# Reading the moving columns of TensorE's matmuls in pairs from both halves, in a float32 attention and feed-forward kernel

## The chip, the cores and the metric

The kernel runs on one core of a Trainium2 chip. The metric is the device time of one execution in microseconds (us). A core has TensorE (PE in the profile; its weight loads stand apart as PEld), VectorE (DVE), ScalarE (ACT), GpSimd (POOL, almost unused here) and SyncE (SP), whose queue issues nearly all DMAs.

## What is computed

```
# q, k, v: (8, 12, 448, 64) float32
scores = q @ k^T / sqrt(64) - log(448)
attn   = 1 / (1 + exp(-scores))                    # sigmoid, no normalisation over keys
x      = (attn @ v), heads side by side            # (3584 tokens, 768)
h      = x @ w_in                                  # 768 -> 2048
g      = s * max(h, 0)**2 + b
out    = g @ w_out                                 # 2048 -> 768
```

All of it is float32. w_in and w_out reach the kernel as 64-bit words, which it converts itself.

## The kernel before

**Precision.** A product of two float32 operands is made from two rounded parts of each, a high and a low part of type float32r, by three matmuls (`PARTS`: high by high, high by low, low by high). A float32r matmul is one record in the trace. Where plain float32 tiles go into a matmul (attention times v, the last 64 keys' scores, the first scores of all), one matmul is two records.

**Attention** runs over 24 steps of `quads`, each with four heads of one batch. `scores` (L420, L426) makes six tiles of 128 keys: the keys are the stationary operand and the 448 queries the moving one, two heads side by side on the two halves of the array's rows. `scores_last` (L441) does the remaining 64 keys for the next step. ACT takes each tile through the sigmoid into an SBUF tile `a`. `attn_v` (L454) and `attn_v_last` (L463) multiply by v, with v stationary and `a` moving, into the PSUM tile `pav`. `store_x` (L470) copies `pav` with DVE, and SP stores it to DRAM as x. `pav` has one buffer, which it shares with the score tile (0, 2) of the next step, the fourth tile in the order in which a step makes them. Beside this, DVE and ACT convert weights, split q and k into parts, and prepare sums of weight blocks, by a plan of numbered steps.

**The first block of 512 tokens** goes through the feed-forward part directly: `ffn1` (L563) and `ffn2` (L765), 18 matmuls each, 16 times in turn, with `activate` on ACT between them. Six PSUM tiles `pos` gather the output and ACT copies them out.

**The other six blocks** are taken three at a time (`threes`), by a scheme of 15 products in place of 18 for a 3 x 2 by 3 x 3 product of blocks. For each of the two groups, a first list of 60 units (L1095: 12 matmuls of 512 columns each) makes sums of h; after each unit `results_1` adds or copies a PSUM tile into the tiles `G`, which are squared and scaled; a second list of 60 units (L1225, again 12 matmuls each) multiplies sums of `G` by sums of w_out; `results_2` (L1138 on) takes each of the 15 finished PSUM tiles into the output tiles `C`, from which SP stores the output. A unit's weights `wu` are fetched from DRAM six units ahead. The last unit is split in three (`LAST`): 512 tokens of one tile, then twice 256 tokens of the other, each with its own subtraction and store.

The order on each engine is written out by hand (the program text is the order); tiles and their releases add the waits. PSUM has four tiles of two banks in the last part, in turn.

**Columns.** In all of these matmuls the moving operand is a row of consecutive 4-byte columns in each partition: `x[r, i, 0, :]`, `two[xi][r, i, :S]`, `x0[h][xi][:, cc, :]`, `g[:, gi, :]`, `opd[i][xi][:, c, :]` and `g[gi][:, f, tk]`. PSUM gets the result's columns in the same order, and so does every tile behind it.

Of the kernel before, what the change touches and what calls it, by code (L numbers as in the profile page):

```python
# [36 lines left out]
TB = 512  # L37
# [57 lines left out]
def sigmoid_attention_relu2_ffn(  # L95
# [10 lines left out]
    nc = tc.nc  # L106
# [66 lines left out]

    def f32(ap):
        return ap.bitcast(F32)

    def add(o, x, y):
        nc.vector.tensor_tensor(o, x, y, op=ALU.add)  # L178

    def sub(o, x, y):  # L180
        nc.vector.tensor_tensor(o, x, y, op=ALU.subtract)  # L181
# [221 lines left out]
    def scores(b, t, ld_):  # L403
        x = ld_[0]
        two = ld_.pop() if len(ld_) > 2 else None
        whole = two is None or (b, t) == quads[0]
        a = {}
        psc = {}
        order = [(i, c) for i in range(2) for c in range(3)]
        if not whole:  # L410
            order[2:4] = order[3], order[2]
        for i, c in order:

            pl, tag = (ps_av, "pav") if (i, c) == (0, 2) else (ps_qk, "psc")
            o = psc[i, c] = pl.tile([P, 2, 512], F32, tag=tag, name=f"psc_{b}_{t}_{i}_{c}")
            if two and (i or not whole):
                cols = slice(S + c * P, S + (c + 1) * P)
                for m, (wi, xi) in enumerate(PARTS):
                    for j, r in enumerate(half):
                        nc.tensor.matmul(  # L420
                            o[:, j, :S], two[wi][r, i, cols], two[xi][r, i, :S],
                            start=m == 0, stop=m == 2,
                        )
            else:
                for j, r in enumerate(half):
                    nc.tensor.matmul(  # L426
                        o[:, j, :S], x[r, i, 1, c * P : (c + 1) * P], x[r, i, 0, :],
                        start=True, stop=True,
                    )
            if not whole and (i, c) == (1, 0):  # L430
                continue
            for k in [(i, c)] + [(1, 0)] * (not whole and (i, c) == (0, 2)):
                a[k] = sigmoid(psc[k], f"{b}_{t}_{k[0]}_{k[1]}")
        return a

    def scores_last(b, t, ld_):
        x = ld_[0]
        psc = ps_qk.tile([P, 2, 512], F32, tag="psc", name=f"psc_{b}_{t}_l")
        for j, r in enumerate(half):
            for i in range(2):  # L440
                nc.tensor.matmul(  # L441
                    psc[half[i], j, :S], x[r, i, 1, 3 * P :], x[r, i, 0, :],
                    start=True, stop=True,
                )
        return sigmoid(psc, f"{b}_{t}_l")
# [21 lines left out]

    def store_x(b, t, pav):
        o = xo.tile([P, 2, S], F32, tag="xo", name=f"xo_{b}_{t}")
        nc.vector.tensor_copy(o, pav[:, :, :S])  # L470
        nc.sync.dma_start(x_dram[b][:, 2 * t : 2 * t + 2], o)

    loaded = {0: load(*quads[0], first=True)}
# [82 lines left out]
    def ffn1(f, w):  # L556
        ph = ps_h.tile([P, TB], F32, tag="ph", name=f"ph_{f}")
        m = 0
        for c in range(NCC):
            h, cc = divmod(c, HC)  # L560
            k, kc = divmod(c, KC)
            for wi, xi in PARTS:
                nc.tensor.matmul(  # L563
                    ph, w[:, k, wi, kc * P : (kc + 1) * P], x0[h][xi][:, cc, :],
                    start=m == 0, stop=m == 3 * NCC - 1,
                )
                m += 1
        cx.free(w)
        return ph
# [191 lines left out]
    def ffn2(w, g, first, last):  # L761
        for e in range(NCC) if not last else evict:
            k, kc = divmod(e, KC)
            for i, (wi, gi) in enumerate(PARTS):
                nc.tensor.matmul(  # L765
                    pos[e], w[:, k, wi, kc * P : (kc + 1) * P], g[:, gi, :],
                    start=first and i == 0, stop=last and i == 2,
                )

# [73 lines left out]
    outs = []  # L843
    for e in evict[::2]:
        outs.append(slot(f"o_{e}"))
        nc.scalar.copy(outs[-1][:, 0], pos[e])
        nc.scalar.copy(outs[-1][:, 1], pos[e + 1])
    todo[10].pop(0)()
    blk_ps.close()
    ps = pool(ctx, "ps", 4, space=PSUM)  # L850
# [100 lines left out]
    for n, blocks in enumerate(threes):  # L951
# [128 lines left out]
        for u, (i, p) in enumerate(L1):  # L1080
            wt = weights()
            if n == 0 and u < 4:
                load_raw(0, *start[5 + u])
            if outs and u > 4:
                out_store(outs[0], evict[6 - 2 * len(outs)], 0, 2)
                heap.free(outs.pop(0))
            ch = next(c for c in CHAINS_1 if i in c)
            if i == ch[0]:
                banks[p] = ps.tile([P, 2, TB], F32, tag="b", name=f"h_{n}_{i}_{p}")
            bk = banks[p]  # L1090
            for j in range(2):
                m = 0
                for c in range(KC):
                    for wi, xi in PARTS:
                        nc.tensor.matmul(  # L1095
                            bk[:, j], wt[:, j, wi, c * P : (c + 1) * P], opd[i][xi][:, c, :],
                            start=i == ch[0] and m == 0,
                            stop=m == 3 * KC - 1,
                            skip_group_check=True,
                        )  # L1100
                        m += 1
            if p == NPP - 1:
                for t in opd.pop(i):
                    heap.free(t)
                for key in {3: ("3",), 13: ("13",), 2: ("2",), 9: ("9",), 5: ("10",), 0: ((0, 2),),
                            12: ((1, 1),), 11: ((1, 2),), 14: ((2, 0),)}.get(i, ()):
                    A.pop(key)
            here = places.get(u, ())
            casts = []
            for q_ in (10,) * (n == 0 and u < 2) + here:  # L1110
                fn = todo[q_].pop(0)
                if u < 4 and fn.__name__ == "hi":
                    casts.append(fn)
                else:
                    fn()
            if u >= len(L1) - LEAD:
                prep(u - len(L1) + LEAD)
            ready, scales = scales, []
            for _ in range(2 - len(here)):
                if later:  # L1120
                    later.popleft()()
            results_1(i, p, bk)
            for fn in casts + ready:
                fn()
            for f, units in LATER_SUMS.items() if n == 0 else ():
                for _ in range(units.count(u)):
                    next(later_sums_[f], None)
# [8 lines left out]
        later = collections.deque()  # L1136

        def results_2(i, bk):  # L1138
            def copy(c):
                C[c] = slot(f"C_{n}_{c}")  # L1140
                nc.scalar.copy(C[c], bk)

            def put(c, keep=False):
                m, k = divmod(c, 3)
# [8 lines left out]
            elif i == 6:  # L1153
                copy(5)
            elif i == 10:
                sub(C[5], C[5], bk)
                put(5)
            elif i == 7:
                C[2] = slot(f"C_{n}_2")
                sub(C[2], C["u"], bk)  # L1160
                copy(0)
                put(2)
            elif i == 1:
                sub(C[0], bk, C[0])
                put(0)
            elif i == 2:
                copy(7)
            elif i == 5:
                copy(8)
            elif i == 4:  # L1170
                sub(C[8], bk, C[8])
            elif i == 3:
                sub(C[7], C[7], bk)
                put(7, True)
            elif i == 12:
                C[1] = C.pop("u")
                sub(C[1], bk, C[1])
                put(1)
            elif i == 11:
                C[3] = slot(f"C_{n}_3")  # L1180
                sub(C[3], C["t"], bk)
                put(3)
            elif i == 14:
                copy("v")
            elif i == 0:
                sub(C["v"], C["v"], bk)

                def eight():
                    add(C[8], C[8], C["v"])
# [9 lines left out]
            elif n + 1 < len(threes):  # L1199
                C[4] = C.pop("t")  # L1200
                for e in range(KC):
                    sub(C[4][:, e], C[4][:, e], bk[:, e])
                    m, k = divmod(4, 3)
                    out_store(C[4][:, e : e + 1], KC * k + e, blocks[m], 1)
                heap.free(C.pop(4))
# [4 lines left out]
        for j, (i, p) in enumerate(L2):  # L1210
# [8 lines left out]
            for e, tk in LAST if end else [(e, slice(TB)) for e in range(KC)]:  # L1219
# [3 lines left out]
                for f in range(2):  # L1223
                    for m, (wi, gi) in enumerate(PARTS):
                        nc.tensor.matmul(  # L1225
                            o, wt[:, f, wi, e * P : (e + 1) * P], g[gi][:, f, tk],
                            start=(end or i == ch[0] and p == 0) and f == 0 and m == 0,
                            stop=p == NPP - 1 and f == 1 and m == 2,
                            skip_group_check=True,
                        )  # L1230
                if end:
                    x = C["t"][:, e, tk]
                    sub(x, x, o)
                    t0 = blocks[1] * TB
                    nc.sync.dma_start(
                        out[(KC + e) * P : (KC + e + 1) * P, t0 + tk.start : t0 + tk.stop], x
                    )
            if n + 1 == len(threes) and j + 2 == len(L2):
                sub(C["t"], C["t"], bk)
            for t in g:  # L1240
                heap.free(t)
            if j in loads:
# [47 lines left out]
```

## Time and profile before

| what | value |
|---|---|
| median of 3 runs | 1039.26 us (1038.59 to 1039.77) |
| span of the profiled execution, first to last instruction | 1037.5 us |
| what lies between that span and the median | 1.8 us |
| ACT busy | 617.2 us (59%) |
| DMA | 287.16 MB, mean 277 GB/s |
| granted TensorE clock, mean | 1.000 |

The profiled execution's time is given by its span alone. "Busy" is time in which an engine had an instruction in it; a matmul's record is longer than the distance to the next, because matmuls are pipelined, so for TensorE the distance between starts counts. A row of a timeline gives the start, the length of the whole group, the engine, the line, what is written and read, the partitions and columns, and how many instructions it merges.

### The profile page before, as it was taken

The numbers are of one execution on the slowest core, as the hardware profiler recorded it, in microseconds if no ns is written. First come the engines' busy times: TensorE is split into PE (matmuls) and PEld (weight loads), VectorE is DVE, ScalarE is ACT, GpSimd is POOL, SyncE is SP. The second block draws the span as 40 slices with busy tenths as digits, with TensorE's granted clock in tenths as the row PEclk, the third lists the DMA queues.
The fourth block names the chain that finished last, engine by engine and source line by source line (L and its number), as shares of the span: only waits on it lengthen the run. The fifth ranks groups of instructions, "written<-read, shape, count | busy, mean of one in ns | idle before, by whom it ended". The sixth has DMA issues, their size and how long they took to land.

```text
span 1037.5 us, 13898 instructions
## 1 busy us (share of the span) xinstructions
PE 1033.7 (100%) x5288; PEld 780.3 (75%) x5288; DVE 836.1 (81%) x906; ACT 617.2 (59%) x666; POOL 0.2 (0%) x4
## 2 busy tenths in 40 slices
PE   9999999999999999999999999999999999999998
PEld 4545555555888888888888888888888888888887
DVE  5999999995988965898898897796455789888777
ACT  7999999988776755564445344344445335552432
POOL 0000000000000000000000000000000000000000
PEclk9999999999999999999999999999999999999999
DMA  9788989995999999999686676897666666676773
GB/s 327 269 331 342 360 317 393 346 396 194 332 366 367 358 408 410 341 341 322 201 269 189 218 229 220 291 317 249 197 190 195 194 193 197 190 236 207 222 228 118
DMA packets 101568, 287.16 MB, mean 277 GB/s; under 512 B 10240, under 2 KB 20352, under 8 KB 101504
## 3 DMA queue, kind: packets, MB, share of 16 engines
q1 hardware_dynamic: 101216, 285.84, 79.6%
q8 instruction: 42, 0.69, 0.3%
q10 hardware_dynamic: 288, 0.46, 0.1%
q14 instruction: 22, 0.18, 0.0%
HBM read 198.18 MB, written 88.08 MB: 276 GB/s over the span
## 4 chain that ended last, share of the span: by engine, by line
PE 100%; DVE 0%; issue 0%
PE o L1225 31%; PE h L1095 31%; PE pav L454 11%; PE psc L420 9%; PE ph L563 6%; PE po L765 6%; PE psc_l L441 2%; PE pav L463 2%; PE psc L426 0%; PE idle L482 0%; DVE C_t L181 0%
## 5 line engine op out<-in xcount | busy, mean ns | idle before, releaser
L1095 PE MATMUL h<-s_1h,wu 128*128 128x512 f32 x480 | 148.0, 389 | 0.0
L1095 PE MATMUL h<-s_0h,wu 128*128 128x512 f32 x480 | 147.8, 389 | 0.0
L400 ACT ACTIVATE a<-psc,nls 128x896 f32<-128x896 f32 x144 | 132.7, 1008 | 12.9 <-PE psc L420 10.1
L454 PE MATMUL pav<-a,v 128*64 128x448 f32 x576 | 113.8, 543 | 0.0
L1095 PEld LDWEIGHTS h<-s_1h,wu 128*128 128x128 f32 x480 | 90.1, 188 | 18.8
L1095 PEld LDWEIGHTS h<-s_0h,wu 128*128 128x128 f32 x480 | 90.1, 188 | 18.6
L968 ACT COPY G<-h 128x1024 f32<-128x1024 f32 x48 | 48.8, 1017 | 85.5 <-PE h L1095 57.8
L860 ACT ACTIVATE G<-G,b_sb,s_sb 128x1024 f32<-128x1024 f32 x48 | 59.8, 1246 | 61.4 <-DVE G L857 60.7
L1095 PE MATMUL h<-s_0l,wu 128*128 128x512 f32 x240 | 93.4, 389 | 0.0
L1095 PE MATMUL h<-s_1l,wu 128*128 128x512 f32 x240 | 93.4, 389 | 0.0
L454 PEld LDWEIGHTS pav<-a,v 128*64 128x64 f32 x576 | 39.1, 137 | 63.8 <-issue 45.4
L178 DVE TENSOR_TENSOR G<-G,h 128x1024 f32<-128x1024 f32 x40 | 48.8, 1219 | 39.4 <-PE h L1095 39.3
L1225 PE MATMUL o<-g_3h,wu 128*128 128x512 f32 (+1 forms) x244 | 79.0, 385 | 0.0
L1225 PE MATMUL o<-g_0h,wu 128*128 128x512 f32 x240 | 78.8, 389 | 0.0
L1225 PE MATMUL o<-g_1h,wu 128*128 128x512 f32 x240 | 78.8, 389 | 0.0
L1225 PE MATMUL o<-g_2h,wu 128*128 128x512 f32 x240 | 78.8, 389 | 0.0
L765 PE MATMUL po<-g,w 128*128 128x512 f32 x288 | 67.7, 389 | 0.0
L765 PEld LDWEIGHTS po<-g,w 128*128 128x128 f32 x288 | 54.1, 188 | 11.2
L563 PE MATMUL ph<-x0h,w 128*128 128x512 f32 x192 | 61.7, 390 | 0.0
L420 PE MATMUL psc<-qkh 64*128 64x448 f32 x282 | 54.1, 380 | 0.0
L1225 PEld LDWEIGHTS o<-g_3h,wu 128*128 128x128 f32 x244 | 45.6, 188 | 9.2
L1095 PEld LDWEIGHTS h<-s_0l,wu 128*128 128x128 f32 x240 | 45.0, 188 | 9.4
(152 smaller groups left out, 2028.0 us busy)
## 6 DMA issues: line engine op xcount, KB each, us to landing
wu<-wd SPq DMA_DIRECT2D x240, 512.0 KB, 3.6
wd<-t SPq DMA_DIRECT2D x36, 768.0 KB, 8.6
qk<-qk_t SPq DMA_DIRECT2D x23, 896.0 KB, 7.4
st<-w_out SPq DMA_DIRECT2D x16, 768.0 KB, 10.3
st<-w_in SPq DMA_DIRECT2D x16, 768.0 KB, 9.3
wd<-w SPq DMA_DIRECT2D x16, 768.0 KB, 5.6
v<-v_t SPq DMA_DIRECT2D x24, 448.0 KB, 6.1
xd<-xo SPq DMA_DIRECT2D x24, 448.0 KB, 4.9
```

The costliest lines, as they stand in the source:

```text
L178: nc.vector.tensor_tensor(o, x, y, op=ALU.add)
L400: nc.scalar.activation(a, psc[:, :, :S], AF.Sigmoid, bias=nls, scale=SCALE)
L420: nc.tensor.matmul(o[:, j, :S], two[wi][r, i, cols], two[xi][r, i, :S], start=m == 0, stop=m == 2,)
L441: nc.tensor.matmul(psc[half[i], j, :S], x[r, i, 1, 3 * P :], x[r, i, 0, :], start=True, stop=True,)
L454: nc.tensor.matmul(pav[r, i, :S], ld_[1][:, 3 * i + c, j, :], a[i, c][:, j, :], start=c == 0, stop=False,)
L463: nc.tensor.matmul(pav[r, i, :S], ld_[1][half[i], 6, j, :], a[half[i], j, :], start=False, stop=True,)
L563: nc.tensor.matmul(ph, w[:, k, wi, kc * P : (kc + 1) * P], x0[h][xi][:, cc, :], start=m == 0, stop=m == 3 * NCC - 1,)
L765: nc.tensor.matmul(pos[e], w[:, k, wi, kc * P : (kc + 1) * P], g[:, gi, :], start=first and i == 0, stop=last and i == 2,)
L860: nc.scalar.activation(x, x, AF.Identity, bias=b_sb, scale=s_sb)
L968: nc.scalar.copy(g(m, h), bk)
L1095: nc.tensor.matmul(bk[:, j], wt[:, j, wi, c * P : (c + 1) * P], opd[i][xi][:, c, :], start=i == ch[0] and m == 0, stop=m == 3 * KC - 1, sk ...
L1225: nc.tensor.matmul(o, wt[:, f, wi, e * P : (e + 1) * P], g[gi][:, f, tk], start=(end or i == ch[0] and p == 0) and f == 0 and m == 0, stop ...
```

## The change

Every moving operand named above, except that of attention times v, is handed to the matmul through `paired`: a view of n columns in the order 0, n/2, 1, n/2 + 1, 2, and so on. The stationary operands, the PSUM addresses and the number of matmuls stay. So PSUM holds the columns in the new order:

- scores come out in this order once, and so do `a` and `pav`, whose matmuls still read consecutive columns. `store_x` puts them back: its DVE copy reads PSUM with a step of two elements (`turned(.., 2)`) and writes consecutive elements, in two runs.
- h comes out in this order, and everything elementwise on `G` and `g` stays in it. The second product reads `g` in pairs again, so its output is turned twice. The copies and subtractions that take the output from PSUM (`results_2`, the `pos` copies, the subtractions of the last unit) read PSUM with a step of four elements and write consecutive ones, in four runs of 128.
- the two halves of the last tile now hold two runs of 128 tokens each, so their stores write two runs of 128 columns per row in place of one of 256.

No instruction is added, removed or moved: on each engine the same operations on the same tiles stand in the same order, with the same semaphores in between. Only access patterns differ.

```diff
+    def paired(ap):
+        return ap.rearrange("p (a b) -> p b a", a=2)
+
+    def runs(ap, n):
+        return ap.rearrange("p j (a b) -> p j a b", a=n)
+
+    def turned(ap, n):
+        return ap.rearrange("p j (b a) -> p j a b", a=n)
...
-                            o[:, j, :S], two[wi][r, i, cols], two[xi][r, i, :S],
+                            o[:, j, :S], two[wi][r, i, cols], paired(two[xi][r, i, :S]),
...
-                        o[:, j, :S], x[r, i, 1, c * P : (c + 1) * P], x[r, i, 0, :],
+                        o[:, j, :S], x[r, i, 1, c * P : (c + 1) * P], paired(x[r, i, 0, :]),
...
-                    psc[half[i], j, :S], x[r, i, 1, 3 * P :], x[r, i, 0, :],
+                    psc[half[i], j, :S], x[r, i, 1, 3 * P :], paired(x[r, i, 0, :]),
...
-        nc.vector.tensor_copy(o, pav[:, :, :S])
+        nc.vector.tensor_copy(runs(o, 2), turned(pav[:, :, :S], 2))
...
-                    ph, w[:, k, wi, kc * P : (kc + 1) * P], x0[h][xi][:, cc, :],
+                    ph, w[:, k, wi, kc * P : (kc + 1) * P], paired(x0[h][xi][:, cc, :]),
...
-                    pos[e], w[:, k, wi, kc * P : (kc + 1) * P], g[:, gi, :],
+                    pos[e], w[:, k, wi, kc * P : (kc + 1) * P], paired(g[:, gi, :]),
...
-        nc.scalar.copy(outs[-1][:, 0], pos[e])
-        nc.scalar.copy(outs[-1][:, 1], pos[e + 1])
+        for k in range(2):
+            nc.scalar.copy(runs(outs[-1], 4)[:, k], pos[e + k].rearrange("p (b a) -> p a b", a=4))
...
-                            bk[:, j], wt[:, j, wi, c * P : (c + 1) * P], opd[i][xi][:, c, :],
+                            bk[:, j], wt[:, j, wi, c * P : (c + 1) * P],
+                            paired(opd[i][xi][:, c, :]),
...
         def results_2(i, bk):
+            bk = turned(bk, 4)
+
+            def c4(c):
+                return runs(C[c], 4)
+
             def copy(c):
                 C[c] = slot(f"C_{n}_{c}")
-                nc.scalar.copy(C[c], bk)
+                nc.scalar.copy(c4(c), bk)
...
-                sub(C[5], C[5], bk)
+                sub(c4(5), c4(5), bk)
...
-                            o, wt[:, f, wi, e * P : (e + 1) * P], g[gi][:, f, tk],
+                            o, wt[:, f, wi, e * P : (e + 1) * P], paired(g[gi][:, f, tk]),
...
-                    x = C["t"][:, e, tk]
-                    sub(x, x, o)
-                    t0 = blocks[1] * TB
-                    nc.sync.dma_start(
-                        out[(KC + e) * P : (KC + e + 1) * P, t0 + tk.start : t0 + tk.stop], x
-                    )
+                    x = C["t"][:, e]
+                    dst = out[(KC + e) * P : (KC + e + 1) * P, blocks[1] * TB : (blocks[1] + 1) * TB]
+                    if tk.stop - tk.start == TB:
+                        x4 = x.rearrange("p (a b) -> p a b", a=4)
+                        sub(x4, x4, o.rearrange("p (b a) -> p a b", a=4))
+                    else:
+                        h = tk.start * 2 // TB
+                        x, dst = (y.rearrange("p (d h b) -> p h d b", d=2, h=2)[:, h] for y in (x, dst))
+                        x4 = x.rearrange("p d (a b) -> p d a b", a=2)
+                        sub(x4, x4, o.rearrange("p (b d a) -> p d a b", d=2, a=2))
+                    nc.sync.dma_start(dst, x)
```

The other branches of `results_2` change in the same way as the one shown.

More of the change, by code (lines that the diff above doesn't have):

```diff
@@ L1159, in results_2 @@
                 C[2] = slot(f"C_{n}_2")
-                sub(C[2], C["u"], bk)
+                sub(c4(2), c4("u"), bk)
                 copy(0)
@@ L1163, in results_2 @@
             elif i == 1:
-                sub(C[0], bk, C[0])
+                sub(c4(0), bk, c4(0))
                 put(0)
@@ L1170, in results_2 @@
             elif i == 4:
-                sub(C[8], bk, C[8])
+                sub(c4(8), bk, c4(8))
             elif i == 3:
-                sub(C[7], C[7], bk)
+                sub(c4(7), c4(7), bk)
                 put(7, True)
@@ L1176, in results_2 @@
                 C[1] = C.pop("u")
-                sub(C[1], bk, C[1])
+                sub(c4(1), bk, c4(1))
                 put(1)
@@ L1180, in results_2 @@
                 C[3] = slot(f"C_{n}_3")
-                sub(C[3], C["t"], bk)
+                sub(c4(3), c4("t"), bk)
                 put(3)
@@ L1185, in results_2 @@
             elif i == 0:
-                sub(C["v"], C["v"], bk)
+                sub(c4("v"), c4("v"), bk)
                 def eight():
@@ L1201, in results_2 @@
                 for e in range(KC):
-                    sub(C[4][:, e], C[4][:, e], bk[:, e])
+                    sub(c4(4)[:, e], c4(4)[:, e], bk[:, e])
                     m, k = divmod(4, 3)
@@ L1231, in sigmoid_attention_relu2_ffn @@
                 if end:
-                    x = C["t"][:, e, tk]
-                    sub(x, x, o)
-                    t0 = blocks[1] * TB
-                    nc.sync.dma_start(
-                        out[(KC + e) * P : (KC + e + 1) * P, t0 + tk.start : t0 + tk.stop], x
-                    )
+                    x = C["t"][:, e]
[9 more added lines that the diff above has]
+                    nc.sync.dma_start(dst, x)
             if n + 1 == len(threes) and j + 2 == len(L2):
-                sub(C["t"], C["t"], bk)
+                ct = runs(C["t"], 4)
+                sub(ct, ct, turned(bk, 4))
             for t in g:
```

## The prediction

> **What bounds the kernel now.** First the head of the page and its chain of waits, followed back from the last instruction.
>
> ```profile
> span 1037.5 us, 13898 instructions
> PE 1033.7 (100%) x5288; PEld 780.3 (75%) x5288; DVE 836.1 (81%) x906; ACT 617.2 (59%) x666; POOL 0.2 (0%) x4
> PE 100%; DVE 0%; issue 0%
> PE o L1225 31%; PE h L1095 31%; PE pav L454 11%; PE psc L420 9%; PE ph L563 6%; PE po L765 6%; PE psc_l L441 2%; PE pav L463 2%; PE psc L426 0%; PE idle L482 0%; DVE C_t L181 0%
> ```
>
> The chain is TensorE alone, so the time is a sum of distances between matmul starts. The lines whose moving operand the change touches and that are float32r (L1225, L1095, L420, L563, L765) hold 83% of it. A busy share of 100% doesn't say that TensorE works at its peak; so next, the same chain in order of time, where rows count matmuls.
>
> ```profile
> 143.15 4.69 PE pav L454 x24
> 153.34 4.69 PE pav L454 x24
> ...
> 259.16 4.08 PE po L765 x18
> 263.24 4.08 PE ph L563 x18
> 381.56 163.20 PE h L1095 x720
> 544.76 163.20 PE o L1225 x720
> 707.96 163.20 PE h L1095 x720
> 871.16 163.28 PE o L1225 x726
> ```
>
> 163.20 us for 720 matmuls is 226.7 ns each, and 4.08 us for 18 is the same number. It is equal in four stages. What splits it is the last unit, which has 256 columns per matmul in place of 512 (columns: start, length, engine, line, operands, shape, count):
>
> ```profile
> 1032.95 0.28 PE L1225 MATMUL o<-g_3l,wu 128*128 128x256 f32 x1
> 1033.07 0.40 PE L1225 MATMUL o<-g_3h,wu 128*128 128x256 f32 x2
> 1033.31 0.28 PE L1225 MATMUL o<-g_3l,wu 128*128 128x256 f32 x1
> ```
>
> From 1032.95 to 1033.31 three matmuls start, 120 ns each. So 256 columns less save 106.7 ns: 0.417 ns for a column, and a matmul of 512 columns costs 213.3 ns for its columns and **13.3 ns that don't depend on their number**. These 13.3 ns are the only thing that another reading order could take away. One reservation: a weight load is as long in both cases, so the 120 ns could be its own limit, and the surplus might then lie in the columns (226.7 over 213.3 is 17 to 16). The amount to be won per matmul of 512 is the same.
>
> Does the surplus come from other engines? The table by stage (busy us and count of PE, PEld, DVE, ACT, POOL; granted clock, DMA share, GB/s) says no:
>
> ```profile
> 350.00:400.00 50.00, 50.00 (x223) 41.38 (x222) 32.64 (x42) 31.54 (x43) 0.00 (x0) 1.00 1.02 387
> 500.00:550.00 50.00, 50.00 (x222) 41.42 (x221) 46.04 (x41) 24.21 (x23) 0.00 (x0) 1.00 0.73 238
> 750.00:800.00 50.00, 50.00 (x222) 41.42 (x221) 27.45 (x23) 24.08 (x23) 0.00 (x0) 1.00 0.66 195
> ```
>
> 222 or 223 matmuls pass in 50 us whether the DMA share is 1.02 or 0.66 and whether DVE is busy for 46.04 or 27.45 us, at a clock of 1.00. So the 13.3 ns are TensorE's own. Is it reading? Attention times v reads plain float32, in two records per matmul, two matmuls at a time on the two halves of the array's columns; here are its weight loads, by twos:
>
> ```profile
> 155.23 0.14 PEld L454 LDWEIGHTS pav<-a,v 128*64 128x64 f32 x2 [0.23 <-ACT a L400]
> ...
> 156.73 0.14 PEld L454 LDWEIGHTS pav<-a,v 128*64 128x64 f32 x2 [0.23 <-issue]
> ```
>
> Four of them in 1.50 us are 375 ns each for 448 columns, twice the 0.417 ns per column (373.3) and some 2 ns. So where columns are taken at half the rate, with 64 weight columns, hardly any surplus is left: it appears where moving columns and 128 weight columns are both read at full rate. The row of the loads shows that they run beside the matmuls nearly all the time, 188 of every 226.7 ns:
>
> ```profile
> L1095 PEld LDWEIGHTS h<-s_1h,wu 128*128 128x128 f32 x480 | 90.1, 188 | 18.8
> ```
>
> This is the reason to think that the reading order matters: two consecutive columns of the new order lie a kilobyte apart, so the stream of columns meets the stream of weights, and itself, in other places of the memory. No row shows what that does.
>
> **The change, part by part.** (1) *Float32r feed-forward matmuls.* With 512 columns there are 1440 in L1095, 288 each in L563 and L765 (16 times 18), and 720 + 714 in L1225, whose last stage has 12 narrow ones among its 726: in all 3450. Bounds per matmul: at best the whole 13.3 ns goes, 3450 x 13.3 = 46 us; at worst every column costs a second step, 213.3 ns, 736 us more. Between ends so far apart I take the value nearest to a row with slower reading, L454's 2 to 3 ns left: 10.7 ns saved, 3450 x 10.7 = **36.9 us**.
>
> [...]
>
> (2) *Float32r scores* (columns as above; the tile (0, 2) starts at 161.55):
>
> ```profile
> L420 PE MATMUL psc<-qkh 64*128 64x448 f32 x282 | 54.1, 380 | 0.0
> L420 PE MATMUL psc<-qkh,qkl 64*128 64x448 f32 x282 | 51.5, 362 | 0.0
> L420 PE MATMUL psc<-qkl,qkh 64*128 64x448 f32 x282 | 51.5, 362 | 0.0
> ...
> 160.33 0.37 PE L420 MATMUL psc<-qkh 64*128 64x448 f32 x2
> ...
> 161.55 0.36 PE L420 MATMUL psc<-qkh 64*128 64x448 f32 x2
> ...
> 162.36 0.37 PE L420 MATMUL psc<-qkl,qkh 64*128 64x448 f32 x2
> ```
>
> 846 matmuls are 423 pairs; ten pairs start in 2.03 us, 203 ns each, 16 over the 186.7 of 448 columns. The same 10.7 ns would save 423 x 10.7 = 4.5 us, 0.19 us per step; at best 16 ns, 6.8 us; at worst 423 x 186.7 = 79 us are added. What may cap the gain is ACT:
>
> ```profile
> 18.00:250.00 232.00, 232.00 (x1728) 123.69 (x1728) 208.67 (x246) 218.09 (x228) 0.00 (x0) 1.00 0.90 335
> ```
>
> ACT is busy for 218.09 of 232 us, 94%. A step of the attention is 10.19 us (143.15 to 153.34 above), of which 6%, 0.6 us, are free, more than 0.19; I take 3 us of the 4.5.
>
> (3) *Plain float32 scores* (L441, L426): their columns are read at half the rate, as in L454, so I take nothing; together they are some 2% of the span, so doubling would cost 20 to 25 us, but then (1) costs far more.
>
> (4) *DVE's and ACT's turned PSUM reads.* Nearest rows:
>
> ```profile
> L470 DVE COPY xo<-pav x24: 1091/1092/1094, 17.0 to 250.8; 128x896 f32<-128x896 f32 x24
> L181 DVE TENSOR_TENSOR t<-t 128x768 fp32r<-128x768 f32 x36 | 33.3, 952 | 0.0
> L215 DVE SCALAR_TENSOR_TENSOR st<-st 128x768 f32<-128x768 uint32 x32 | 30.7, 960 | 0.8
> L1141 ACT COPY C<-o x8: 1014/1016/1022, 577.4 to 969.2; 128x1024 f32<-128x1024 f32 x8
> ```
>
> L215 reads words two elements apart in SBUF and takes 960 ns, against 952 for consecutive ones: nothing below and above worth counting. For a step of four elements in PSUM there is no row; the bounds are nothing and a doubling. The 30 reads of `results_2`, 1.0 us each on ACT and a little more on DVE, would then grow by that much. A list of 60 units has 15 of them in 163.20 us, one per 10.9 us, and the tile isn't written again before another product has run, so these 10.9 us cover it. The six `pos` copies, half the size of L1141's, would grow by 0.5 us each, at worst 3 us, once. I take 0 for all of it. Rival E below prices the exception, `store_x`.
>
> (5) *What is late next.* With 36.9 of 3450 x 226.7 ns = 782 us gone, each 50 us of work must fit in 47.6. DVE's 46.04 in 500 to 550 just fits, and the DMA share of 1.02 in 350 to 400 becomes the limit for that stretch; six units of prefetch at 2.7 us each are 16 us of cover, against 2.3 us of lag. I take 1.5 us back for such waits.
>
> (6) *The end.*
>
> ```profile
> 1034.46 0.42 DVE L181 TENSOR_TENSOR C_t<-C_t,o 128x256 f32<-128x256 f32 x1 [0.30 <-PE o L1225]
> ```
>
> This last subtraction could double too, and its store writes two runs where it wrote one; I take 0, at worst 0.5 us.
>
> Sum: 36.9 + 3 - 1.5 = 38.4 us off the profiled span of 1037.5, so 999.1; the median shown lies 1.8 us above that span, so **1001 us**.
>
> **The rivals.**
>
> *B, nothing happens.* The 13.3 ns may be the switch from one set of weights to the next, which no reading order touches: every matmul here has its own weight load, and L454, where the surplus is missing, loads 64 columns, not 128. That speaks for B as strongly as for the forecast. Then 1039.
>
> *C, the pairs are slower to read.* If consecutive columns are fetched several at a time, alternating ones need a fetch of their own for each column. If that can't be had every 0.417 ns, a column takes two steps: 736 + 79 us, so 1039 + 815 = about 1854 us, in every stage alike. The point of decision is low: more than 13.3 ns in 512 columns, 0.026 ns per column, loses time. For it: the surplus hangs on the full rate, so reading has little to spare, and no float32r matmul in the trace reads with a step. Against it: L215 loses nothing by reading apart, though its rate, 768 elements in 960 ns, is a third of TensorE's.
>
> [...]
>
> *E, the attention's copy.* The PE side gains nothing, and L470 doubles from 1.09 to 2.18 us. It starts right after the step's last matmul:
>
> ```profile
> 159.76 1.09 DVE L470 COPY xo<-pav 128x896 f32<-128x896 f32 x1 [0.43 <-PE pav L463]
> ```
>
> It ends at 160.85 now; the tile (0, 2), which needs its buffer, starts at 161.55. So from 1.8 us on TensorE waits; at 2.18 it waits 0.4 us, 24 times, 10 us: 1049. The row L215 speaks against it.
>
> **How the numbers follow.** Forecast 0.56, B 0.16, C 0.2, E 0.08. I keep C at 0.2, because only the absence of a row stands against it. The forecast's own range runs from all of 13.3 and 16 ns gone (46 + 6.8 us: 986) to small gains near 1030. The range takes in B and E, and leaves out C: 986 to 1052. A measurement of this kernel can tell some 0.2% (2 us) from no change: faster 0.56, same 0.16 (B), slower 0.28 (C and E).
>
> **What would show it.** Right: in the chain by time, the four long stages fall from 163.20 to about 155.5 us and the rows of 18 from 4.08 to 3.89, while L454's 24 stay near 4.69. B: 163.20 again. C: these rows near 317 us. E: L470 over 1.8 us and waits of TensorE on it. If the long stages shorten but the span doesn't follow, TensorE has idle time released by DVE or DMA. If rows of 512 fall to 213.3 ns, the whole surplus was reading.

## The result, and the profile after

| | before | changed |
|---|---|---|
| median | 1038.92 us (1038.31 to 1039.77, 4 runs) | 1011.61 us (1010.77 to 1011.83, 4 runs) |
| ratio | 1 | 0.9735, 95% interval 0.9721 to 0.9749 |
| span of the profiled execution | 1037.5 us | 1010.1 us |

The change is 27.3 us faster; the forecast was 1001 us, 38 us faster, with a range of 986 to 1052. Here are the head of the page of the changed kernel, its chain by engine, and then rows of its chain in order of time (start, length, what, how many):

```profile
span 1010.1 us, 13900 instructions
PE 1001.0 (99%) x5288; PEld 784.2 (78%) x5288; DVE 837.1 (83%) x906; ACT 616.7 (61%) x666; POOL 0.2 (0%) x4
PE 77%; ACT 8%; DVE 6%; DMA 5%; issue 3%; SPq 1%; ACTq 0%; DVEq 0%
```

```profile
144.89 4.73 PE pav L463 x24
155.20 4.73 PE pav L463 x24
253.67 7.97 PE ph L572 x36
273.50 3.88 PE ph L572 x18
397.75 142.06 PE h L1104 x648
695.84 155.40 PE h L1104 x720
851.24 155.66 PE o L1240 x726
```

The count of 13900 is two above that of before: TensorE's sequencer has two more semaphore waits, while matmuls, weight loads, DVE and ACT have as many instructions as they had. Three things are to be seen. First, the long stages run at 155.40 us for 720 matmuls, 215.8 ns each in place of 226.7, and 18 matmuls take 3.88 us. Second, the step of the attention got longer: 144.89 to 155.20 is 10.31 us, where it was 10.19. Third, the chain isn't TensorE alone any more: 8% is ACT, 6% DVE, 5% DMA, and the first list is cut in two (648 of its 720 matmuls come behind a gap).

The account, by the rows above and those of before: the feed-forward part began at 250.73 and now begins at 253.67, 2.9 us later. Its first row in the chain of the kernel before:

```profile
250.73 8.43 PE ph L563 x36
```

From there to the end of its last row (1034.44 before, 1006.90 now) it took 783.7 us and takes 753.2, 30.5 less. Together 27.5 us, against 27.4 by the spans. But 3450 matmuls at 10.8 ns less are 37.4 us: the feed-forward part **gave back 7 us**, and the attention lost 3 where 3 were to be won.

The gap in the first list, from the timelines of TensorE and ACT:

```profile
394.35 0.38 PE L1104 MATMUL h<-s_0h,wu 128*128 128x512 f32 x1
397.75 0.48 PE L1104 MATMUL h<-s_0h,wu 128*128 128x512 f32 x1 [3.01 <-ACT G L977]
```

```profile
395.74 1.05 ACT L687 CAST s_0h<-a 128x1024 fp32r<-128x1024 f32 x1 [5.12 <-DMA a<-xd]
396.69 1.92 ACT L977 COPY G<-h 128x1024 f32<-128x1024 f32 x2
```

TensorE waits for ACT's copy out of PSUM. Ahead of that copy in ACT's order is a split of a token tile `a`, and ACT had stood before it for 5.12 us, because DMA had not brought the tile. The table by stage shows DMA and the clock there, first in the changed kernel, then in the one before:

```profile
360.00:380.00 20.00, 20.00 (x94) 17.50 (x94) 13.63 (x20) 10.42 (x15) 0.00 (x0) 1.00 1.05 385
380.00:400.00 20.00, 16.99 (x77) 14.47 (x76) 9.47 (x8) 12.40 (x16) 0.00 (x0) 0.98 1.05 408
400.00:420.00 20.00, 20.00 (x87) 16.99 (x86) 13.47 (x17) 9.61 (x11) 0.00 (x0) 0.94 1.01 392
```

```profile
380.00:400.00 20.00, 20.00 (x90) 16.53 (x89) 11.60 (x10) 13.79 (x17) 0.00 (x0) 1.00 1.05 407
```

The DMA share is 1.05, and it was 1.05 before as well, with no gap: DMA moves no more bytes per time than it did (408 and 407 GB/s), while TensorE asks for them sooner. Behind the gap the mean clock of 0.94 means 87 matmuls in 20 us where 94 went through before it. So the gap costs 3.2 us itself and some 1.7 us at a reduced clock; smaller waits (the longest 0.5 us) make up the rest of the 7 us.

What didn't change is the turned reading of PSUM:

```profile
L479 DVE COPY xo<-pav x24: 1090/1091/1093, 17.5 to 253.7; 128x896 f32<-128x896 f32 x24
L1156 ACT COPY C<-o 128x1024 f32<-128x1024 f32 x8 | 8.1, 1016 | 37.1 <-PE o L1240 34.5 <-DVE C L190 2.6
```

1091 ns and 1016 ns, as before: a step of two elements in PSUM cost DVE's copy nothing, and a step of four cost ACT's copy nothing. DVE's subtractions of `results_2`, with a step of four, take 1.22 us in both kernels.

### The profile page after: what moved, and what is told of

Read it like the earlier page. It is cut to its first block, busy times and chain, and to the rows that moved or that the text cites. A ratio compares the mean times of both kernels' runs of the same rounds, so it can differ in the third digit from the quotient of the medians.

```text
span 1010.1 us, 13900 instructions
## 1 busy us (share of the span) xinstructions
PE 1001.0 (99%) x5288; PEld 784.2 (78%) x5288; DVE 837.1 (83%) x906; ACT 616.7 (61%) x666; POOL 0.2 (0%) x4
## 4 chain that ended last, share of the span: by engine, by line
PE 77%; ACT 8%; DVE 6%; DMA 5%; issue 3%; SPq 1%; ACTq 0%; DVEq 0%
PE o L1240 30%; PE h L1104 29%; PE pav L463 9%; ACT a L409 5%; DMA a<-xd 2%; PE psc_l L450 2%; PE ph L572 2%; DVE t L190 2%; PE pav L472 2%; PE psc L429 1%; PE po L774 1%; DVE w L190 1%; DMA wd<-w 1%; DMA wd<-t 1%; ACT wf L215 1%
## 5 line engine op out<-in xcount | busy, mean ns | idle before, releaser
L1104 PE MATMUL h<-s_0h,wu 128*128 128x512 f32 x480 | 144.7, 382 | 3.0 <-ACT G L977 3.0
L1104 PE MATMUL h<-s_1h,wu 128*128 128x512 f32 x480 | 142.9, 379 | 0.0
L1104 PE MATMUL h<-s_1l,wu 128*128 128x512 f32 x240 | 91.0, 379 | 0.0
L1240 PE MATMUL o<-g_3h,wu 128*128 128x512 f32 (+1 forms) x244 | 76.4, 376 | 0.0
L1240 PE MATMUL o<-g_2h,wu 128*128 128x512 f32 x240 | 76.3, 379 | 0.0
L1240 PE MATMUL o<-g_0h,wu 128*128 128x512 f32 x240 | 76.3, 379 | 0.0
L1240 PE MATMUL o<-g_1h,wu 128*128 128x512 f32 x240 | 76.3, 379 | 0.0
L187 DVE TENSOR_TENSOR G<-G,h 128x1024 f32<-128x1024 f32 x40 | 48.7, 1218 | 31.6 <-PE h L1104 30.5
L774 PE MATMUL po<-g,w 128*128 128x512 f32 x288 | 65.1, 380 | 0.5 <-DVE g L190 0.5
```

What stands on the lines that cost most here:

```text
L774: nc.tensor.matmul(pos[e], w[:, k, wi, kc * P : (kc + 1) * P], paired(g[:, gi, :]), start=first and i == 0, stop=last and i == 2,)
L1104: nc.tensor.matmul(bk[:, j], wt[:, j, wi, c * P : (c + 1) * P], paired(opd[i][xi][:, c, :]), start=i == ch[0] and m == 0, stop=m == 3 * KC ...
L1240: nc.tensor.matmul(o, wt[:, f, wi, e * P : (e + 1) * P], paired(g[gi][:, f, tk]), start=(end or i == ch[0] and p == 0) and f == 0 and m == ...
```

## The experiments

**1. The reading orders alone.** Streams of 24 matmuls (48 records in plain float32), each matmul with its own weight load, in one order each.

```diff
+    run("plain", m0, full)
+    run("pairs", turned(m0, 2), full)                 # 0, 256, 1, 257, ...
+    run("quarters", turned(m0, 4), full)              # 0, 128, 256, 384, 1, ...
+    run("near_b", near(m0, 2, 4), full)               # 0, 4, 1, 5, 2, 6, 3, 7, 8, ...
+    run("step_b", step(m0, 2), full)                  # 0, 2, 4, ..., then 1, 3, ...
+    run("step_d", step(m0, 4), full)                  # 0, 4, 8, ...
+    run("twos", m0.rearrange("p (a b c) -> p b a c", a=2, c=2), full)   # 0, 1, 256, 257, ...
...
+    run("plain_nw", m0, narrow, 512, 64)              # 64 weight columns
...
+    run("plain_half", m[:, :256], full, 256)
...
+    run("plain_ff", raw[:, 0, :512], plain32)         # plain float32
```

> Streams of 24 matmuls alone, each with its own weight load; the rest of the computation is left out. Distance between starts. Theory T (the 13.3 ns is a clash of the stream of columns with something read beside it, fixed per matmul): plain float32r 226.7 ns at 512 columns, pairs 215.8; with 64 weight columns in place of 128 plain falls by about half of the surplus (220); 256 plain with 64 weight columns 113 or less; 384 plain 173.3. Theory R (consecutive 4-byte columns are read at 16/17 of the full rate): plain 512 stays 226.7 with 64 weight columns, 384 takes 170, 256 with 64 weight columns 113.3. Theory W (the 120 ns of 256 columns are the weight load's own limit): 256 falls well below 120 with 64 weight columns. bf16 is 215.8 in both orders under all. [...] Plain float32 on the whole array: pairs slower than plain by about a quarter, if what slowed the last 64 keys' scores (376 to 473 ns) is the pair reading of plain float32; no difference, if it needs the four tiles side by side, which the last two streams have.

The timeline of TensorE, one row per stream; the distance from a row's start to the next one's, over the count, is the time of a matmul (the last matmul of a stream in another shape than the next blurs it by a few ns). `near_c` and `near_d` have the two columns of a pair 16 and 64 columns apart, `nw` is 64 weight columns, `half` 256 and `most` 384 moving columns, `ff` plain float32.

```profile
20.51 5.34 PE L47 MATMUL bf_plain<-movb,stab 128*128 128x512 bf16 x23
25.69 11.79 PE L47 MATMUL bf_pairs<-movb,stab 128*128 128x512 bf16 x24
36.86 6.08 PE L47 MATMUL plain<-mov,sta 128*128 128x512 f32 x24
42.77 5.34 PE L47 MATMUL pairs<-mov,sta 128*128 128x512 f32 x24
47.95 6.96 PE L47 MATMUL quarters<-mov,sta 128*128 128x512 f32 x24
54.74 5.35 PE L47 MATMUL near_b<-mov,sta 128*128 128x512 f32 x24
59.93 5.34 PE L47 MATMUL near_c<-mov,sta 128*128 128x512 f32 x24
65.11 5.34 PE L47 MATMUL near_d<-mov,sta 128*128 128x512 f32 x24
70.29 10.99 PE L47 MATMUL step_b<-mov,sta 128*128 128x512 f32 x24
81.10 11.25 PE L47 MATMUL step_d<-mov,sta 128*128 128x512 f32 x24
92.17 8.34 PE L47 MATMUL twos<-mov,sta 128*128 128x512 f32 x24
100.34 5.64 PE L47 MATMUL plain_late<-mov,sta 128*128 128x512 f32 x24
105.81 5.68 PE L47 MATMUL plain_nw<-mov,sta 128*64 128x512 f32 x24
111.33 5.34 PE L47 MATMUL pairs_nw<-mov,sta 128*64 128x512 f32 x24
116.51 3.04 PE L47 MATMUL plain_half<-mov,sta 128*128 128x256 f32 x24
119.39 2.84 PE L47 MATMUL pairs_half<-mov,sta 128*128 128x256 f32 x24
122.07 2.91 PE L47 MATMUL plain_half_nw<-mov,sta 128*64 128x256 f32 x24
124.81 2.78 PE L47 MATMUL pairs_half_nw<-mov,sta 128*64 128x256 f32 x24
127.43 4.36 PE L47 MATMUL plain_most<-mov,sta 128*128 128x384 f32 x24
131.63 4.32 PE L47 MATMUL plain_most_nw<-mov,sta 128*64 128x384 f32 x24
135.79 20.76 PE L47 MATMUL plain_ff<-raw,wraw 128*128 128x512 f32 x48
156.39 26.08 PE L47 MATMUL pairs_ff<-raw,wraw 128*128 128x512 f32 x48
182.40 4.74 PE L102 MATMUL four_plain<-raw,wraw 64*64 64x448 f32 x48
```

By these rows, in ns per matmul of 512 columns: pairs 216, whether the two columns lie 4, 16, 64 or 256 apart; consecutive columns 246 in `plain`, which starts slowly behind the bf16 pairs, and 228 in `plain_late` (227 once either runs); twos 340; quarters 283; steps of two 450, of four 461; bf16 pairs 465 (484 once they run), where bf16 in consecutive order takes 216 (one of its 24 records is missing). What this says of the three theories:

- *The reading order does it, with the same weight loads.* Pairs in place of consecutive columns save 11 ns of a matmul of 512 columns with 128 weight columns, and 14 with 64 (230 to 216).
- *Theory T falls at 512 columns.* It put the surplus down to a clash with the weight load. With 64 weight columns, whose loads are shorter (137 ns for L454's in the kernel before, 188 for L1095's), consecutive reading takes 230 ns, no less than with 128.
- *Theory W falls too.* 256 consecutive columns take 120 ns with 128 weight columns and 114 with 64, so the wider load costs something there. But in pairs, with the same loads of 128 weight columns, they take 112, so 120 is not the load's own limit. The last unit of the changed kernel agrees: three matmuls of 256 columns start in 0.33 us, 110 ns each, where it was 120.

```profile
1005.50 0.28 PE L1240 MATMUL o<-g_3l,wu 128*128 128x256 f32 x1
1005.61 0.39 PE L1240 MATMUL o<-g_3h,wu 128*128 128x256 f32 x2
1005.83 0.28 PE L1240 MATMUL o<-g_3l,wu 128*128 128x256 f32 x1
```

- *Theory R, a lower rate for consecutive columns, fits half of the rows.* Over 0.417 ns per column, 256, 384 and 512 consecutive columns have a surplus of some 7, 13 and 17 ns with 64 weight columns, which grows as R says (7, 10 and 13), though faster. With 128 weight columns it is 13, 15 and 13, as if it were fixed. No single one of the theories gives both series. What makes consecutive columns slow stays open.
- *Plain float32 pays for pairs.* 429 ns per record become 542 (540 once they run), a quarter more, on the whole array and without other tiles beside it. In consecutive order they have next to no surplus with 128 weight columns either: 429 is twice 213.3 and 2.5 ns.

**2. Feed-forward in pairs, attention as before.**

```diff
-                            o[:, j, :S], two[wi][r, i, cols], paired(two[xi][r, i, :S]),
+                            o[:, j, :S], two[wi][r, i, cols], two[xi][r, i, :S],
...
-        nc.vector.tensor_copy(runs(o, 2), turned(pav[:, :, :S], 2))
+        nc.vector.tensor_copy(o, pav[:, :, :S])
```

> The attention reads and copies as before the change, the feed-forward part in pairs. Theory (the attention lost 0.114 us per step by its pairs, above all in the last 64 keys' scores): a step is 10.19 us again, the feed-forward matmuls stay at 215.8 ns, 1011.6 - 24 x 0.114 = 1008.9 us. Rival (the attention's loss has another cause, such as another placement of tiles): steps stay at 10.31, 1011.6.

1008.45 us (ratio 0.9707, 0.969 to 0.9723), and steps of 10.19 us. The theory holds.

**3. Attention in pairs, feed-forward as before.**

```diff
-                            o[:, j, :S], two[wi][r, i, cols], two[xi][r, i, :S],
+                            o[:, j, :S], two[wi][r, i, cols], paired(two[xi][r, i, :S]),
...
-        nc.vector.tensor_copy(o, pav[:, :, :S])
+        nc.vector.tensor_copy(runs(o, 2), turned(pav[:, :, :S], 2))
```

> Only the attention in pairs, the feed-forward part as before. Theory: steps of 10.31 us, feed-forward matmuls 226.7 ns, 1038.9 + 2.7 = 1041.7 us. Rival (the attention's pairs gain, and lose only by what the faster feed-forward part brings with it): about 1038.9 - 5 = 1034.

1041.81 us (ratio 1.0025, 1.0016 to 1.0035), steps of 10.31 us, 163.20 us per long stage. The attention's part of the change is a loss of 2.7 us by itself.

**4. Only the plain float32 scores back in consecutive order.** Their PSUM tile then has the queries in plain order, and ACT's sigmoid reads it in pairs, so that `a` comes out in the order of the others.

```diff
-                    psc[half[i], j, :S], x[r, i, 1, 3 * P :], paired(x[r, i, 0, :]),
+                    psc[half[i], j, :S], x[r, i, 1, 3 * P :], x[r, i, 0, :],
...
+        if turn:
+            o = a.rearrange("p j (b a) -> p j b a", a=2)
+            x = x.rearrange("p j (a b) -> p j b a", a=2)
+        nc.scalar.activation(o, x, AF.Sigmoid, bias=nls, scale=SCALE)
```

> As changed, but the scores of the last 64 keys read consecutive columns, and ACT's sigmoid reads their PSUM tile in turned order instead. Theory: these eight records take 0.80 us per step again in place of 0.99, a step is 10.12 us, 1011.6 - 24 x 0.19 = 1007.1 us. Rival (ACT sets the pace of a step, so that what is saved there is waited for elsewhere): steps of 10.2 to 10.3, 1009 to 1011.6.

1007.72 us (0.9697, 0.9683 to 0.9712), and steps of 10.12 us. The group of eight records, in the timelines of the kernel before, of the changed kernel and of this one:

```profile
157.96 0.98 PE L441 MATMUL psc_l<-qk 64*64 64x448 f32 x8
```

```profile
149.55 1.17 PE L450 MATMUL psc_l<-qk 64*64 64x448 f32 x8
```

```profile
156.35 0.98 PE L454 MATMUL psc_l<-qk 64*64 64x448 f32 x8
```

1.17 us fall to 0.98, what the group took before the change. The theory holds. Run again it gave the same time:

> The version with only the last 64 keys' scores in plain order once more, beside it on the same chip: 1007.7 us under both.

1007.34 us (0.9694, 0.9681 to 0.9708). It is the fastest version that computes everything, 31.6 us under the kernel before and 4 us under the changed one. The six float32r score tiles alone, then, gain less than their matmuls do. In the changed kernel (timelines of TensorE and ACT):

```profile
151.41 0.46 PE L429 MATMUL psc<-qkh 64*128 64x448 f32 x2
...
155.20 0.97 PE L463 MATMUL pav<-a,v 128*64 128x448 f32 x4
```

```profile
152.34 4.60 ACT L409 ACTIVATE a<-psc,nls 128x896 f32<-128x896 f32 x5 [0.55 <-PE psc L429]
```

`pav` needs the buffer of the tile (0, 2), whose sigmoid is the third. Sigmoids start at 152.34 and follow each other at 0.92 us (4.60 over 5); the third is over at 155.1, and `pav` starts at 155.20. So the section from the first score to `pav`, 3.79 us where it was 3.87 (159.62 to 163.49), is now ACT's, and of the 18 x 13 ns that the pairs of matmuls save per step only 0.08 us arrive.

**5 and 6. The split of a token tile three units later,** with the fix of experiment 4, and in the kernel before.

```diff
-        0: (13,), 1: (13, 2), 2: (13, 2), 3: (2, 1), 4: (1,), 5: (8,), 6: (8,), 7: (8,), 8: (8,),
-        9: (12,), 10: (12,), 11: (12,), 12: (12, 7), ...
+        0: (13,), 1: (13, 2), 2: (13, 2), 3: (2,), 6: (1,), 7: (1, 8), 8: (8,), 9: (8, 12),
+        10: (8, 12), 11: (12,), 12: (12, 7), ...
```

> As the version with the last 64 keys' scores in plain order, and product 1's split of its tokens (first needed in unit 20) moves from units 3 and 4 to 6 and 7, product 8's jobs by two units, so that ACT doesn't stand in unit 3 before a token tile that DMA has not brought yet. Theory (the stall of 3.8 us near 390 us and the nine matmuls at half clock behind it are ACT's wait for that tile, ahead of the copy that frees PSUM): both go, 3.6 + 1.9 = 5.5 us, 1007.7 - 5.5 = 1002.2 us. Rival (DMA is full in 360 to 410 us, so the same time is waited for at the next load, such as a unit's weights): at most 1 us is won, and TensorE idles behind a DMA between 390 and 420 us.

> The kernel before with the same move of jobs alone. Theory (the wait was hidden before the change, because 12 matmuls of 226.7 ns leave more time): no change, 1039.1 us within 1 us. Rival (the move helps by itself): 1034.

Experiment 6: 1039.83 us (ratio 1.0008, 0.9998 to 1.0017), no change. Experiment 5 **missed**: 1010.96 us (0.9728, 0.9713 to 0.9742), 3 us slower than experiment 4. The gap near 390 us went, and a longer one came at 406 us (timeline of DVE, then who waited for whom):

```profile
406.57 0.69 DVE L190 TENSOR_TENSOR t_e<-wr 128x512 f32<-128x512 f32 x1 [5.97 <-DMA wr<-wr]
```

```profile
PEld h L1107 <- DVE G L187: 6.4, 1, 6.4
```

Now DVE stood for 5.97 us before a reloaded weight block, ahead of the addition that frees PSUM. The rival was right, only the load is another than it named.

**7 and 8. The sums from reloaded weight blocks four units later; then also the first block's output stores later.**

The other three rows of the table move in the same way.

```diff
-    4: (6, 9, 9, 10, 11, 11, 11, 12, 13, 13, 14, 14),
+    4: (6, 13, 13, 14, 15, 15, 15, 16, 17, 17, 18, 18),
...
-            if outs and u > 4:
+            if outs and u > 12:
```

> As the version with the later split, and the sums made from reloaded weight blocks (wr) start four units later, while their load stays in unit 6 for the first. Theory (in 360 to 410 us DMA is full at over 400 GB/s, and each engine that stands in its order before a late load stops the PSUM release behind it; with the consumers of both late loads moved, TensorE waits for neither): the stall of 6.4 us and its ten matmuls at half clock go, 1011.0 - 6.2 - 2.1 = 1002.7 us. Rival (the bytes are what is missing, so the unit's own weights wu come late next): a stall of 3 us or more stays between 400 and 430 us, now on wu; 1006 to 1011.

> The same, and the stores of the first block's output (three of 512 KB) wait until unit 13 in place of 5. Under the theory 1002.7 as well, or up to 0.5 less; under the rival it takes 1.5 MB, 3.7 us at 410 GB/s, out of the full stretch and is faster than the run without it by up to 3 us.

Both **missed**: 1009.0 us (0.9711, 0.9696 to 0.9725) and 1013.39 us (0.9755, 0.9739 to 0.9771). The long gap went; in its place came several waits for DVE between 408 and 505 us, of 0.3 to 1.8 us in experiment 7 and of up to 2.3 us in experiment 8. The moved sums now stand there among the additions of later units; that they are the cause is argued from their place, no run separates it. The stores that wait until unit 13 fall into the same stretch, and the version with them is slower.

**9 and 10. Only the first of the sums later; then the same without storing the first block's output.**

```diff
-    4: (6, 9, 9, 10, 11, 11, 11, 12, 13, 13, 14, 14),
+    4: (6, 12, 12, 13, 14, 14, 14, 15, 15, 16, 16, 17),
...
-                out_store(outs[0], evict[6 - 2 * len(outs)], 0, 2)
```

> As the version with the later split, and only the first of the four sums made from reloaded weight blocks is used three units later (its load stays in unit 6, the other three sums stay where they are). Theory (two waits at the head of DVE's and ACT's orders for late loads, and nothing else, make up what was given back near 400 us): no stall over 1 us in the first list, 1011.0 - 8.4 = 1002.6 us. Rival (in this stretch the bytes are the limit, so that a wait only changes its place): one or several stalls of some 4 to 7 us in all stay, 1006 to 1009.

> As the run before it with one of the sums later, but the first block's output (three stores of 512 KB, issued from 395 us on) is not stored; this part of the output is left out. Theory (the stretch from 360 to 420 us is short of DMA bytes per time): 1.5 MB are 3.7 us at 410 GB/s; the stall of 3.3 us at 418 us and the half clock behind it go or shrink to under 1 us, 1007.9 - 5 = 1003 us. Rival (only the place of jobs in the orders of ACT and DVE counts, not the bytes): the stall stays, 1007 to 1008.

Experiment 9: 1007.87 us (0.9703, 0.969 to 0.9717), what experiment 4 had, with a gap of 3.3 us at 418: the rival. Experiment 10: 1005.11 us (0.9678, 0.9662 to 0.9695), 2.8 us less; the gap of 3.3 us is gone, two of under 1 us stand at 421 and 424. Stages of experiment 9, then of 10, and what ACT stood before in experiment 9, then in 10:

```profile
410.00:420.00 10.00, 8.48 (x40) 7.05 (x38) 4.30 (x8) 3.13 (x4) 0.00 (x0) 1.00 1.03 417
```

```profile
410.00:420.00 10.00, 10.00 (x49) 8.74 (x48) 6.11 (x10) 6.50 (x9) 0.00 (x0) 1.00 0.83 292
```

```profile
419.42 1.06 ACT L693 ACTIVATE s_0h<-a 128x1024 fp32r<-128x1024 f32 x1 [5.06 <-DMA wd<-t_e]
```

```profile
416.06 1.06 ACT L693 ACTIVATE s_0h<-a 128x1024 fp32r<-128x1024 f32 x1 [1.76 <-DMA wd<-t_e]
```

With 1.5 MB less, the DMA share falls below 1 in this stretch (0.83) and 49 matmuls pass in place of 40. The profile puts ACT's wait down to the same thing in both, a store of a sum (`wd<-t_e`). SP issues it at 413.03 in experiment 9 and at 412.97 in experiment 10; it lands 6.0 us later in the one and 3.0 us later in the other. So neither the order on the queue nor another tile explains the shorter wait: the transfer itself is faster.

Three versions in which jobs changed places (5, 7, 9) each traded the gap for others; taking bytes away removed it. So experiment 9's gap is a shortage of DMA time. That the changed kernel's own gap at 394 us is the same shortage is argued, from the DMA share of 1.05 there and from the way the gap moves when jobs move; no run took bytes out ahead of it. The win was 2.8 us of the 5 expected, as the two small gaps stayed; what would remove those wasn't tried.

## Why the prediction was right, and where its terms were off

- **The bound** (TensorE alone, a sum of distances between starts) and **the forecast's mechanism** were right: reading in pairs takes most of the 13.3 ns off. Term (1) was 10.7 ns and 36.9 us; measured are 10.8 ns and 37.4 us. Float32r pairs of 512 columns take 215.8 ns, as consecutive bf16 does in experiment 1. That the term came out so near is partly luck. Its 10.7 ns were borrowed from L454, the nearest row between bounds far apart, and nothing shows that the 2 to 3 ns left there and those left in pairs have one cause.
- **The reason given for it was wrong.** The prediction has "13.3 ns that don't depend on their number", from rows of 512 and 256 columns with 128 weight columns. Experiment 1 gives 13, 15 and 13 ns for such rows, but 7, 13 and 17 with 64 weight columns, so it is not one fixed amount. The reservation beside it, that the 120 ns could be the weight load's own limit, doesn't hold either: pairs take 112 with the same loads. And the prediction tied the surplus to "128 weight columns", since L454 with 64 had hardly any. L454 differs from the others in type as well, and it is the type that counts: float32r with 64 weight columns has 17 ns, plain float32 with 128 has 2.5. So at 512 columns the clash with the weight load that the forecast leaned on isn't the cause. What the memory does with consecutive 4-byte columns stays open; the runs show rates only.
- **Term (2), scores.** The matmuls gave more than expected (a pair takes 189 ns, some 13 less, in place of 10.7) and the step kept 0.08 of 0.24 us. "What may cap the gain is ACT" was right, but the cap was looked for in ACT's total (94% busy), and it lies in the first score tile and the three sigmoids behind it, 3.79 us to the start of `pav`, against 3.87 before.
- **Term (3), plain float32 scores, taken at nothing, was mis-sized:** "their columns are read at half the rate" was no protection. They cost 0.19 us per step, 24 x 0.19 = 4.5 us, and turned the attention's part into a loss (experiments 3 and 4).
- **Term (4), turned PSUM reads:** right, no cost.
- **Term (5), what is late next: 1.5 us predicted, 7 us measured.** This term made most of the difference between forecast and result. The stretch was named (DMA share 1.02 in 350 to 400), but its lag was set against the cover of the unit weights, and TensorE never waited for those. Late were a token tile, then reloaded blocks and a store, whose consumers stand in ACT's and DVE's orders ahead of the PSUM release (waits of 5.12 us in the changed kernel, 5.97 in experiment 5 and 5.06 in experiment 9); and behind the gap the granted clock was lower (0.94 in 400 to 420 us), which no term had.
- **The rivals.** B: the long stages didn't stay at 163.20. E: the copy took 1091 ns, so TensorE never waited on it. C: no float32r stage slowed, yet its price is real for other orders and types (steps of two 450 ns, bf16 pairs 484, plain float32 pairs a quarter more). Its 0.2 was the author's estimate, made without a row of a float32r matmul that reads with a step; experiment 1 has such rows now. How far apart the columns lie doesn't sort them: pairs take 216 ns at 4, 16, 64 and 256 columns, and steps of two and four 450 and 461. The measurement decides.

In sums: 37.4 + 1.9 (scores) - 4.5 (plain float32 scores) - 7 = 27.8 us, against 27.3 measured. The forecast was 38: its largest term came out, terms (2), (3) and (5) all missed in the same direction, and the range of 986 to 1052 was wide enough to take in no change at all.

## What to carry to other kernels

When a kernel is one engine from end to end, a few percent can sit in the order in which operands are read (here 215.8 ns for 226.7), and a stream of two dozen instructions by themselves shows it; but the order that is best for one type can cost a quarter or double for another (here plain float32, 540 ns for 429, and bf16, 484 for 215.8), so each type is measured. A surplus per instruction is only called fixed, or put down to a cause, after size, weights and type have been varied one at a time; here one series looked fixed (13, 15 and 13 ns) and the other grew (7, 13 and 17). And where the bound engine gets faster, look at each stretch in which another resource is already full (here DMA, with a share of 1.05): loads were late here, each behind the engine that stood in order before it (ACT for 5.12 us in the changed kernel, DVE for 5.97 in experiment 5), and moving jobs about only moved the wait.

## What the runs showed of the hardware that was not expected

- float32r columns in pairs took 215.8 ns per 512, as consecutive bf16 ones did, and consecutive ones 226.7; the distance within a pair made no difference (216 ns at 16, 64 and 256 bytes and at 1 KB). Four places in turn (283 ns), two columns from each of two places (340 ns) and constant steps of two and four (450 and 461 ns) were all slower than consecutive ones.
- bf16 did the opposite: 215.8 ns for consecutive columns, 484 for pairs. Plain float32 went from 429 to 540 ns per record when read in pairs.
- DVE read PSUM with steps of two and of four elements, and ACT with a step of four, at the speed of consecutive ones (1091 ns, 1.22 us and 1016 ns, as before).
- Reading order and the width of the weight load acted together on short matmuls: 256 float32r columns took 120 ns (consecutive, 128 weight columns), 114 (consecutive, 64), 112 (pairs, 128) and 109 (pairs, 64).
- In the changed kernel a gap of 3.2 us on TensorE was followed by some 3.4 us at half the clock (granted clock 0.50 in 400 to 402 us, matmuls 427 ns apart). In experiment 8 a gap of 2.3 us had 35 records of matmuls in 9.43 us behind it, 269 ns each (mean granted clock of the execution 0.998); in experiment 7, with gaps of up to 1.8 us, the clock was 1.00 in each stretch of 20 us from 380 us on.
